# A fused sparse-attention and feed-forward kernel: a new written-out order, one zeroing moved from VectorE to GpSimd, fewer products without use

## The chip, the cores and the metric

The kernel runs on one core of a Trainium2 chip. The core has a matrix engine (TensorE, PE in the profile), VectorE (DVE), ScalarE (ACT), GpSimd (POOL) and SyncE (SP), which each work through their own list of instructions in order and wait for one another by semaphores; DMA queues move data between the memory outside the core (HBM) and its SBUF. Products land in PSUM, which has eight banks. The metric is the device time of one launch in microseconds. Three runs of the kernel before are shown; their median is the time before.

## The reference, cut to what matters

```python
# q, k, v: 4 batches x 8 heads x 768 positions x 64
k_sum = k.reshape(B, H, 24, 32, D).max(axis=3)       # block maxima of the keys
v_sum = v.reshape(B, H, 24, 32, D).mean(axis=3)      # block means of the values
scores_l = scale * q @ k.T                           # only |i - j| < 16 counts
scores_s = scale * q @ k_sum.T + log(32)
a = softmax(concat([where(mask_l, scores_l, -1e9), scores_s]))
x = (a @ concat([v, v_sum])).transpose(0, 2, 1, 3).reshape(3072, 512)
h = x @ w_in                                         # 512 -> 2048
out = (h * clip(h + 3, 0, 6) / 6) @ w_out            # 2048 -> 512
```

All inputs and the output are float32 in HBM; the kernel works in bf16 with float32 sums in PSUM.

## The kernel before

**Tiles and stages.** Of each batch, a block of 64 queries sees a window of 96 keys (its own 64 and 16 to either side) and the 24 block keys: 120 keys, on 120 partitions. So the values of two buffers, `vaug`, have 96 window rows and 24 rows of block means for each of 8 heads and 12 query blocks. The names carry the batch: `V0c` loads the values of head pair c of batch 0 (line 424, on POOL's queue) into rows 32 to 95. The window's first 32 rows are copied from other blocks (`h0cx`, "halo", line 427, x for the half of the query blocks). The block means of batch 0 come from `vsum_first` (`u00` and `u01`, line 612, two head pairs each): 24 products for each pair with a matrix `ind` of zeros and ones, 96 rows by 12 x 32 columns, whose ones mark which block a row belongs to. Rows 0 to 31 of `ind` must be zero, since the halo rows are counted in their own place. The sums are copied to `vf` and spread from there over the query blocks of `vaug`. `blocks()` (line 340) makes `ind` on POOL in three steps, and a DVE memset (line 347) zeroes its first 32 rows.

Keys and queries of a pair are loaded (`K0c`, `Q0..`), transposed on PE (`k0c`, `q0nc` steps, lines 495, 538, 551) and copied out of PSUM by DVE or ACT. A score step `s` (lines 579, 588) makes the scores of a pair in an `S` pair of banks, ACT takes their exponential into `at` (line 597) and DVE multiplies by `mask` (line 601). A value step `v` (lines 709, 711, 713) multiplies by the values and by a column of ones, and a finish step divides (lines 743, 747: reciprocal and scale on DVE into `xn`), transposes on PE (line 781) and copies to `x`. All small copies go through one helper, line 479.

Then, for each of 8 half batches s and 16 column blocks of `w_in`, step F (line 792) makes 4 products of 128 x 384 into a PSUM bank `h` (line 800), a relu on ACT (line 805) and a combined minimum and multiply on DVE into `g` (line 807). For the first half batch and the first blocks the products come in three parts of 128 columns, since the columns of `x` come one after the other. Step G (line 811) sums over the 16 `g` for 128 tokens into bank `o`, or `h` in the last half batch (line 820), copies to `ot` (line 479) and stores (line 832). The last tiles are stored in two halves of 256 columns.

**What sets the order.** All steps are registered with planned costs. A string `ORDER` (line 29) lists every step once, as a name, a running number and, where two engines could do it, the engine (`:A` ACT, `:D` DVE, `:P` POOL, `:S` SP). `Plan.run` (line 156) walks that list with a clock for each engine, the planned costs and the buffers that come free, which gives each step a planned begin and its buffers; the program is then written out in the order of the planned begins. Each engine keeps to its part of that order. The planned costs thus set the order and the choice of buffers, and nothing else. The loads of weights, keys, queries and values all go through POOL's queue; stores go through SP's, and some through POOL's.

**Products without use.** `keep` (line 907) writes products of a constant tile `idle` into a free bank (line 910). The loop behind it (lines 914 to 926) looks at each PE step that is planned before 22 us and puts as many of them ahead as the planned gap holds: by 0.43 us for one in the first 4.5 us, by 0.43 or by 0.216 after that.

Of the kernel before, what the change touches and what calls it, by code (L numbers as in the profile page):

```python
# [43 lines left out]
F13.9 F10.3 F13.10 F10.4 F10.5 F13.11 w13.0 G02.2 F10.9 F11.9 F10.10 F10.11 G02.3 F11.6 F12.3 w10.0 w12.0 w11.0 w12.1:D
G02.4:A F12.4 F11.10 w11.1:A G01.0 G01.1 G01.2 G01.3 u1.0 F11.11 G01.4:A F12.5 w11.2 w13.1:A F11.7 w10.1:A u1.1:A u1.6:A
w10.2 w13.2 w10.3:A u1.4:D F11.8 w13.3:D w11.3:D G00.0 G00.1 G00.2 q100.0 q120.0 q110.0 q100.1:A s100.0 s100.3 s100.1 G00.3
q130.0 q120.1:D q110.1:D w12.2 w12.3:D s100.2 u1.8:D u1.2:D s100.4 q130.1:D K23.0 h11.0 K22.0 h10.0 K21.0 Q21.0 K20.0 Q20.0
Q23.0 Q22.0 V22.0 h21.0 V21.0 h20.0 V20.0 V23.0 G00.4:A s110.0 G00.5 F13.3 G12.0 s110.1 s110.3 s120.0 F13.4 s120.3 s120.1
G12.1 G12.2 F13.5 u1.3:D s120.2 s110.2 h1w.0:A s130.0 s130.1 s130.3 G12.3 G12.4:A G12.5 G01.5 s130.2 s110.4 v10.0 s130.4
v10.1 v10.2 v10.5 v10.6 G11.0 G11.1 v12.0 v10.3 u1.9:A u1.7:A u1.5:A v12.1 v12.2 s120.4 w20.0 w20.3 G11.2 v10.4:A v10.7  # L50
v10.8:A v12.3 v12.4:A G11.3 v15.0 v15.1 v15.2 F20.0 G11.4:A F20.1 F20.3 F20.4 F20.6 v13.0 F20.7 F20.2 F20.5 F20.8 v13.5
v13.1 v13.2 F20.9 F22.0 F21.0 w20.2:A F20.10 F22.1 v13.3 F21.1 F20.11 F22.2 F21.2 w20.1 v13.6 F21.6 F22.6 F21.3 v13.4:A
F21.7 F22.7 v15.3 G10.0 v13.7 F21.4 v15.4:A w20.5:A v13.8:A F21.8 F22.8 F21.5 F22.3 F21.9 w20.4:A F22.4 F21.10 F22.9 G10.1
s200.0 w22.0 w21.0 F22.10 w22.2:A s200.3 s200.1 F22.11 F22.5 w23.0 F21.11 G10.2 F23.6 G10.3 F23.0 F23.3 V30.0 V33.0 V31.0
h30.0 h31.0 V32.0 Q33.0 Q31.0 K33.0 Q32.0 K32.0 Q30.0 K31.0 K30.0 F23.7 w21.2:A w21.1 F23.8 G10.4:A F23.1 w21.5:A F23.4 u2.0
u2.1:A u2.2:A F23.9 w21.3 w21.4:D F23.5 w22.1 F23.2 G10.5 G02.5 F23.10 s210.0 F30.9 G20.0 s210.3 u2.4:A u2.5:D w23.1 F23.11
w22.3 G20.1 F30.0 F30.1 F30.10 s210.1 w22.5:A F30.2 w22.4:D F30.11 u2.3:D G20.2 F30.3 G20.3 F30.4 w23.5:A F30.5 w23.3 s210.2
F30.6 G20.4:A F30.7 s210.4 F30.8 s220.0 w23.2:A s220.3 s220.1 w23.4:A F31.3 F33.3 G22.0 u3.0 F31.4 u3.1:A F33.4 s220.4
s220.2 s200.2 F31.5 F32.6 F32.7 s200.4 F33.5 F32.8 s230.0 G22.1 F31.0 G22.2 h2w.0:A s230.1 s230.3 s230.2 s230.4 F32.3 v20.0
F31.9 F31.1 F31.2 v20.1 v20.4 v20.2 v20.5 u3.5:A F31.10 F31.11 F32.0 G22.3 v22.0 v25.0 v20.3 v22.1 v22.2 v22.3 v20.6 F31.6  # L60
u3.3:A G22.4:A F32.4 F31.7 F32.1 F31.8 F32.5 F32.2 w30.1 v22.5:P v22.7:P G21.0 G21.1 G21.2 F33.6 G21.3 F33.7 G11.5 G20.5:S
v22.6:S v22.4:S F33.8 F33.9 F33.0 F32.9 v25.1 w31.1 v25.2 G21.4:A F33.1 G21.5:P G22.5:S F32.10 F32.11 G32.0 G32.1 G32.2
F33.10 F33.11 F33.2 G32.3 h3w.0:A G32.4:A w30.0 w30.3 w31.5:A w30.2:A u3.4:A v23.0 w31.0 G30.0 G30.1 G30.2 F40.0 F42.9
w30.4:A v23.4 v23.5 v23.1 v23.2 v23.3 v25.3 F40.1 F42.10 F40.3 F40.4 F40.2 F42.11 F41.3 F40.5 v23.6 F40.6 F40.9 F41.4 F40.7
F40.10 F41.5 G30.3 G30.4:A F40.8 F40.11 w31.3 F43.9 w30.5:A F43.10 F41.9 F43.6 F41.10 F43.7 F43.11 F41.11 u3.2:A v25.4:S
v25.7:P v25.6:P G32.5:S v25.5:S G30.5:P G31.0 F41.0 F41.6 F43.8 w31.2:D w31.4:D w33.0 F42.6 F41.7 F41.1 F41.8 F42.7 w32.0
F41.2 F42.8 s310.0 G31.1 s310.3 s310.1 F42.3 G31.2 F43.3 F42.0 F42.4 w32.2:A F43.4 F42.1 F42.5 w32.3 F43.0 F43.1 F43.5 F42.2
# [152 lines left out]
def kernel(  # L220
# [83 lines left out]
    def const_ops():  # L304
# [42 lines left out]
        op("DVE", 0.2, lambda: nc.vector.memset(ind[0:BLK], 0.0), w=["ind"], prio=-78)  # L347
# [609 lines left out]
```

## Time and profile before

| | |
|---|---|
| runs shown, us | 220.47, 220.41, 218.79 |
| median, us | 220.41 |
| profiled execution, us | 218.78 |
| its span, us | 217.1 |
| PE busy, us | 207.0 |
| DVE busy, us | 165.0 |
| ACT busy, us | 136.9 |
| POOL busy, us | 91.0 |
| products without use recorded (line 910) | 17, 7.4 us |
| DVE memset of `ind` (line 347) | 14.16 to 14.38 us |
| V's fourth piece, issue to landing | 9.46 to 17.26 us |
| first product of F | 21.97 us |

The span goes from the first to the last instruction of one profiled execution; the time of that execution is 1.7 us longer. Busy times are of single engines and overlap. Positions are in us from the start of the span. A row such as "A <- B: 1.2, 1, 1.2" among the waits says that A stood idle for B, how long in all, how often, and the longest. A line of the chain has start, length and the work that the end hangs on. The digits show forty equal slices of the span in tenths (9 is 90% or more).

### The profile page before, as it was taken

Reading aid. Unit: us, or ns where it says so; the run is one execution under the profiler, and the core shown is the slowest. Engines: PE = TensorE matmul, PEld = TensorE weight load, DVE = VectorE, ACT = ScalarE, POOL = GpSimd, SP = SyncE. Lnnn points to the kernel's source line nnn. Section 1 sums busy time; section 2 is a strip of 40 time slices with the busy share of each in tenths; the row PEclk is TensorE's granted clock in tenths of the full one; section 3 lists DMA queues with packets and bytes.
Section 4 is the critical chain, followed back from the end, with each engine's and each line's share of the span. In section 5 each row is a group of like instructions: output and inputs, shape, how many; then the busy total and the mean of one; then the engine's idle time right before and its main releaser. Section 6 shows DMA issues by size and latency. Waiting matters only on the chain.

```text
span 217.1 us, 5338 instructions
## 1 busy us (share of the span) xinstructions
PE 207.0 (95%) x2124; PEld 116.4 (54%) x2151; DVE 165.0 (76%) x330; ACT 136.9 (63%) x271; POOL 91.0 (42%) x117
## 2 busy tenths in 40 slices
PE   6979899999999999999999999999999999999994
PEld 2546656554554565555555555545555555555543
DVE  6889999779798899988898898987865756163310
ACT  8687795664789688998844788963342344345301
POOL 7997944254697856527254073000542401100000
PEclk9999999999999999999999999999999999999999
DMA  5999999999999999999936045000540452100212
GB/s 75 159 155 182 205 207 184 168 138 155 106 125 154 190 148 151 131 204 156 107 35 142 0 77 95 3 0 3 130 91 15 107 90 57 51 0 0 97 51 98
DMA packets 129705, 23.03 MB, mean 106 GB/s; under 512 B 120816, under 2 KB 127152, under 8 KB 129680
## 3 DMA queue, kind: packets, MB, share of 16 engines
q0 software_dynamic: 112656, 17.34, 119.2%
q1 hardware_dynamic: 17024, 5.34, 10.1%
q8 instruction: 17, 0.28, 0.5%
q14 instruction: 8, 0.07, 0.1%
HBM read 29.62 MB, written 6.29 MB: 165 GB/s over the span
## 4 chain that ended last, share of the span: by engine, by line
PE 84%; POOL 4%; DMA 4%; DVE 4%; issue 2%; ACT 2%; POOLq 0%
PE h L800 37%; PE o L820 32%; PE h L820 5%; DMA vaug<-in_v_dram 4%; PE S L709 3%; PE S L588 2%; DVE g L807 2%; POOL vaug L424 1%; PE S L641 1%; POOL first L383 1%; PE S L781 1%; DVE at L601 1%; ACT at L597 1%; POOL first L391 1%; ACT ot L479 0%
## 5 line engine op out<-in xcount | busy, mean ns | idle before, releaser
L800 PE MATMUL h<-x,win 128*128 128x384 bf16 (+1 forms) x536 | 94.3, 319 | 1.3 <-DVE g L807 1.3
L807 DVE SCALAR_TENSOR_TENSOR g<-r,h 128x384 bf16<-128x384 f32 x128 | 67.6, 547 | 29.8 <-ACT r L805 27.5
L805 ACT ACTIVATE r<-h 128x384 f32<-128x384 f32 x128 | 60.6, 492 | 45.9 <-PE h L800 44.4
L820 PE MATMUL o<-wout,g 128*128 128x512 bf16 x312 | 79.0, 379 | 1.6 <-issue 0.5
L800 PEld LDWEIGHTS <-win 128*128 128x128 bf16 x536 | 49.6, 98 | 36.5 <-issue 1.9
L820 PEld LDWEIGHTS <-g 128*128 128x128 bf16 x400 | 38.0, 98 | 36.7
L769 POOL DMA_DIRECT2D x<-y x28 | 17.2, 622 | 40.9 <-issue 22.0
L597 ACT ACTIVATE at<-S 120x768 bf16<-120x768 f32 x32 | 24.7, 813 | 2.4 <-PE S L588 2.4
L424 POOL DMA_DIRECT2D vaug<-in_v_dram x16 | 15.1, 945 | 13.0 <-issue 3.9
L479 ACT COPY ot<-o 128x512 f32<-128x512 f32 x18 | 10.6, 587 | 13.0 <-PE o L820 12.0
L601 DVE TENSOR_TENSOR at<-at,mask 96x768 bf16<-96x768 bf16 x28 | 14.5, 547 | 2.2 <-ACT at L597 1.8
L747 DVE TENSOR_TENSOR xn<-S,rc 128x512 bf16<-128x512 f32 (+1 forms) x24 | 15.7, 661 | 0.5
L413 POOL DMA_DIRECT2D kraw<-in_k_dram x8 | 10.7, 1339 | 8.2 <-issue 4.2
L479 ACT COPY vaug<-vs 24x1536 bf16<-24x1536 bf16 (+1 forms) x10 | 12.1, 1212 | 0.2
L678 DVE TENSOR_REDUCE red<-kaug 128x24 bf16<-128x768 bf16 x12 | 11.1, 941 | 0.1
L820 PE MATMUL h<-wout,g 128*128 128x256 bf16 (+1 forms) x63 | 10.7, 325 | 0.1
L832 POOL DMA_DIRECT2D out_dram<-ot x7 | 4.0, 567 | 14.0 <-DVE ot L479 8.5
L588 PEld LDWEIGHTS <-kaug 64*128 64x128 bf16 x384 | 6.8, 95 | 5.5 <-issue 3.3
L709 PEld LDWEIGHTS <-at 120*64 120x64 bf16 x360 | 6.8, 111 | 4.5 <-issue 3.7
L588 PE MATMUL S<-qT,kaug 64*128 64x64 bf16 x384 | 8.8, 191 | 0.2 <-ACT qT L479 0.2
L910 PE MATMUL o<-idle 128*128 128x512 bf16 x17 | 7.4, 572 | 1.6 <-DVE idle L306 1.5
L709 PE MATMUL S<-vaug,at 120*64 120x65 bf16 x352 | 8.2, 197 | 0.1
(107 smaller groups left out, 181.9 us busy)
## 6 DMA issues: line engine op xcount, KB each, us to landing
vaug<-in_v_dram POOLq DMA_DIRECT2D x22, 192.0 KB, 11.1
out_dram<-ot SPq DMA_DIRECT2D x14, 256.0 KB, 3.1
win<-in_moe_w_in_dram POOLq DMA_DIRECT2D x4, 512.0 KB, 8.5
wout<-in_moe_w_out_dram POOLq DMA_DIRECT2D x4, 512.0 KB, 14.5
kraw<-in_k_dram POOLq DMA_DIRECT2D x8, 192.0 KB, 13.8
out_dram<-ot POOLq DMA_DIRECT2D x5, 256.0 KB, 2.4
first<-in_k_dram POOLq DMA_DIRECT2D x6, 192.0 KB, 6.3
first<-in_q_dram POOLq DMA_DIRECT2D x6, 192.0 KB, 9.0
```

What stands on the lines that cost most here:

```text
L424: op("POOL", 0.95, lambda: nc.gpsimd.dma_start(out=o[BLK:WIN, lo:hi, 0:D], in_=rows[:, lo:hi]), w=[("v", b % 2, c)], prio=prio, dma=1.25, ...
L479: {"ACT": nc.scalar.copy, "DVE": nc.vector.tensor_copy, "POOL": nc.gpsimd.tensor_copy}[eng](o, i)
L588: nc.tensor.matmul(X[p, half].slot[:, j, i * QB:(i + 1) * QB], kaug[p][rows, t], qT[rows, p, t * QB:(t + 1) * QB], start=not masked, stop= ...
L597: op("ACT", act(2 * HALF), lambda a=a, x=x: nc.scalar.activation(a, x.slot[0:KEYS, :, 0:HALF], AF.Exp, scale=scl), r=[x], w=[("at", p, hal ...
L601: op("DVE", 0.57, lambda m=m, half=half: nc.vector.tensor_tensor(m, m, mask[:, low(half):low(half) + HQ].unsqueeze(1).to_broadcast([WIN, 2 ...
L709: nc.tensor.matmul(y, a[:, cols], vaug[b % 2][0:KEYS, h, t, 0:D + 1], start=True, stop=True)
L747: nc.vector.tensor_tensor(o, src[..., 0:D], r.unsqueeze(len(r.shape)).to_broadcast(list(o.shape)), op=ALU.mult)
L769: QUEUE[eng].dma_start(out=xt[s].slot[32 * a:32 * a + 32].rearrange("p k (t c j) -> p (k t) c j", t=3, c=4)[:, :, c], in_=ys[s].slot[32 * ...
L800: nc.tensor.matmul(h.slot[:, lo * 128:hi * 128], w_in_sb[:, kt, ft * 128:(ft + 1) * 128], xt[s].slot[:, kt, lo * 128:hi * 128], start=(kt ...
L805: op("ACT", act(HALF), lambda: nc.scalar.activation(r.slot[:], h.slot[:, 0:HALF], AF.Relu, bias=0.5, scale=1.0 / 6.0), r=[h], w=[r], prio= ...
L807: op("DVE", dve(HALF), lambda: nc.vector.scalar_tensor_tensor(gt[s].slot[:, ft], r.slot[:], 1.0, h.slot[:, 0:HALF], op0=ALU.min, op1=ALU.m ...
L820: nc.tensor.matmul(o.slot[:, a:z], gt[s].slot[:, ft, ts * 128:(ts + 1) * 128], w_out_sb[:, ft, a:z], start=(ft == 0), stop=(ft == NFT - 1))
```

## The change

The list is written anew from its first token. In the first 25 us: all small memsets (`z`, `e`) stand ahead of the constant tile `idle` (`c.0`) on DVE; the first sums `u00` stand ahead of the last scores of the start and take a bank `h`; `h030` and `h020` are both ahead of `u01`; `h011` is on ACT; `u00.6` (a spread of block means) is behind the third `g`; `q011` is ahead of `q031`; the edges of the second `vaug` (before `c.9`, after `c.8`) come earlier. Later steps and the stores of the last tiles are in a different order too, and some copies and stores are on another engine.

`blocks()` has a third POOL step behind its two selects, a memset of the first 32 rows of `ind`, in place of the DVE step, so that the numbers of the `c` steps behind it go down by one. The planned DVE costs of a halo copy and of the spread's second half are larger. `keep`'s rule for the time after 7.2 us is dropped, so that all gaps after 4.5 us are filled by 0.43 us less 0.4, and no product without use stands ahead of the sums. The program then has 13 of them instead of 19. The numbers of all products with use are as before.

```diff
--- before.py
+++ after.py
@@ -27,59 +27,59 @@
 
 
 ORDER = """
-c.0 z1.0:A z3.1:A z0.1:A K00.0 z1.1:D e.3 z0.2 z2.0:D c.8 K01.0 c.1 K02.0 Q000.0 c.2 Q010.0 c.3 k00.0 z0.0:D e.1 z3.0:D c.4
-k01.0 V00.0 V01.0 V02.0 V03.0 c.6 Q01w2.0 Q01w1.0 I0.0 Q01w0.0 k01.2:A k00.1 e.0 k01.1 z2.2 z3.2 z2.1:D k01.4 z1.2 k03.0
-k00.3:A k00.2:A k01.3:A q010.0 q010.1:A q000.0 k02.0 q000.1:A k00.4 s000.0 q030.0 s010.0 q020.0 s000.1 s010.1 e.2 k03.1
-k02.1 h000.0:D h001.0:D k03.4 c.7 q020.1:D k03.3:A q030.1:A k03.2:A s000.2 s010.2 Q11w0.0 I1.0 I2.0 u00.0 k02.4 h010.0:D
-u00.2:A k02.2:A h021.0:D h020.0:D u00.1:D u00.3:D u00.5:D h030.0:D s030.0 s030.1 s020.0 s020.1 s030.2 u01.0 s020.2 I3.0 O0.0
-O1.0 K13.0 O2.0 O3.0 K11.0 K10.0 K12.0 u01.2:A u01.1:A v00.0 v01.0 v02.0 v01.1 v00.2 v00.3 v02.2 v02.3 v01.2 v01.3 v00.1
-v00.6 v02.1 v00.4 v00.5 v02.4 v02.5 k02.3:A v00.7:A u00.4:A v01.4 v00.8 v00.9:A v01.5:A v02.6 v02.7:A F00.0 F00.10 F00.1
-q021.0 q001.0 F00.2 q021.1:A h011.0:D u00.6:D h031.0:D u01.3:D q001.1:D F00.3 F00.11 F00.12 q031.0 F00.4 F00.5 F00.6 F00.7
-F00.15 q031.1:A F00.13 F00.8 F00.16 c.5 F00.14 F00.9 F00.17 u01.4:D s031.0 q011.0 s031.1 q011.1:A F01.6 F01.7 s031.2 F01.8
-F01.3 F01.4 F01.0 F01.1 F01.5 c.9 F01.2 s001.0 s011.0 s011.1 s011.2 s001.1 s001.2 F02.0 F02.9 F02.1 F02.2 s021.0 F01.9
-F02.10 F02.11 F03.0 F02.3 s021.1 F01.10 s021.2 F03.1 F01.11 v03.0 v04.0 F03.2 v03.1 v04.1 v04.2 v03.2 F03.6 F03.9 G02.0
-v03.3 v05.0 F02.4 F03.10 F03.7 F02.5 F03.8 v05.1 v05.2 F02.6 v03.4:A F02.7 v04.3 F03.3 v04.4:D Q11w3.0 V13.0 V12.0 V10.0
...
-F73.2 F70.9 F70.6 F70.7 F70.8 F72.0 G60.2 F72.1 F70.10 F70.11 F72.2 F73.6 F73.7 F73.8 G60.3 G60.4:A F71.9 F72.6 F72.7 F71.10
-F71.11 F72.8 G61.0 F70.3 F70.4 F70.5 G61.1 F73.9 F73.10 F73.11 F71.0 F71.1 F71.6 F71.7 F71.8 F71.2 G61.2 F72.3 F72.4 G61.3
-G70.0 G61.4:A F72.5 G62.5:P G61.5:S G71.1 G71.3 F73.3 F73.4 G70.1 G70.2 F73.5 G60.5:S G70.3 G72.0 G72.1 G70.4:D G70.5 G71.5
-G72.2 G72.3 G71.0 G71.2 G72.4:A G72.5 G71.9 G71.10:D G71.11 G71.4 G71.6 G71.7:A G71.8
+z2.2 z1.2 z3.2 e.3 e.0 c.0 z1.1:D z0.1:A z1.0:A z3.1:A K00.0 c.7 z0.0:D z2.0:D z3.0:D e.1 z0.2 K01.0 c.1 K02.0 Q000.0 c.2
+Q010.0 c.3 k00.0 c.4 k00.1 e.2 k00.4 k01.0 V00.0 V01.0 V02.0 V03.0 c.6 Q01w2.0 Q01w1.0 I0.0 Q01w0.0 k01.2:A k01.1 k01.4
+z2.1:D k03.0 k00.2:A k00.3:A k01.3:A k02.0 k02.2:A k03.1 k03.4 q010.0 q000.0 q010.1:A q000.1:A s010.0 q020.0 q030.0 k03.3:A
+q030.1:A s000.0 s010.1 s000.1 u00.0 s010.2 s000.2 k03.2:A k02.1 k02.4 h000.0:D h001.0:D q020.1:D h010.0:D u00.2:D u00.5:D
+h021.0:D u00.1:A u00.3:D h030.0:D h020.0:D Q11w0.0 I1.0 I2.0 s020.0 s020.1 s030.0 s030.1 u01.0 s020.2 s030.2 I3.0 O0.0 O1.0
+K12.0 O2.0 O3.0 K10.0 K13.0 K11.0 u01.1:A u01.2:A v00.0 v01.0 v02.0 v01.1 v00.2 v00.3 v02.2 v02.3 v00.6 v00.1 v01.2 v01.3
+v00.4 v00.5 v02.1 v02.4 v02.5 u00.4:A k02.3:A v00.7:A h011.0:A v01.4 v00.8 v00.9:A v01.5:A v02.6 v02.7:A F00.10 F00.0 F00.1
+q021.0 q001.0 F00.2 F00.11 F00.12 F00.5 q021.1:A h031.0:D u01.3:D u01.4:D q001.1:D F00.3 F00.13 q011.0 F00.6 q011.1:A q031.0
+F00.7 c.5 F00.8 q031.1:A F00.4 c.8 F00.14 F00.9 F00.15 s001.0 s031.0 F00.16 s031.1 u00.6:D F00.17 F01.6 F01.7 s031.2 F01.8
+F01.3 F01.4 s011.0 F01.0 F01.5 s001.1 s001.2 F02.0 F02.9 s021.0 F01.1 F01.2 F02.1 F02.2 s011.1 s011.2 F02.10 F02.11 F02.3
+F01.9 F03.0 s021.1 F01.10 s021.2 F03.1 F01.11 v04.0 v03.0 v04.1 F03.2 v03.1 v04.2 v03.2 F03.6 F03.9 G02.0 v05.0 v03.3 F03.7
...
+F70.8 F72.6 F72.7 F73.3 F73.4 F73.5 F72.0 F72.1 F72.2 F72.8 G60.3 F71.0 F71.9 G60.4:A F71.1 F71.2 F71.6 F71.7 F71.8 G61.0
+F70.3 F73.0 G61.1 G61.2 F70.4 F73.1 F73.2 F71.10 F70.5 F70.9 F70.10 F70.11 F71.11 G61.3 F73.9 F72.3 F72.4 G72.0 G72.1 F72.5
+F73.10 G62.5:S G61.4:A G61.5:P G60.5:P F73.11 G70.0 G72.2 G71.1 G71.3 G71.5 G71.9 G71.10:D G71.11 G51.5:P G70.1 G72.3
+G72.4:D G72.5 G71.0 G70.2 G70.3 G70.4:D G70.5 G71.2 G71.4 G71.6 G71.7:A G71.8
 """
 
 BANKS = ("S", "h", "o")
@@ -343,8 +343,8 @@
                                     pattern=[[QB, NQ], [-BLK, 32]])
             nc.gpsimd.affine_select(out=ind[:], in_=ind[:], compare_op=ALU.is_ge, fill=0.0, base=2 * BLK - 1, channel_multiplier=-1,
                                     pattern=[[-QB, NQ], [BLK, 32]])
-        op("POOL", 1.6, blocks, w=["ind"], prio=-78.5)
-        op("DVE", 0.2, lambda: nc.vector.memset(ind[0:BLK], 0.0), w=["ind"], prio=-78)
+            nc.gpsimd.memset(ind[0:BLK], 0.0)
+        op("POOL", 1.85, blocks, w=["ind"], prio=-78.5)
 
         def edges(i):
             t = vaug[i]
@@ -434,7 +434,7 @@
             copy(eng, o[0:BLK, hs, a:z, 0:D], o[QB:WIN, hs, a - 1:z - 1, 0:D])
             if x:
                 copy(eng, o[0:BLK, hs, 0, 0:D], o[QB:WIN, hs, NQ - 1, 0:D])
-        op(EITHER, {"ACT": 0.75 + 0.1 * x, "DVE": 0.42 + 0.1 * x}, go, r=[("v", 0, c), ("vz", 0, c)], w=[("vh", 0, c, x)],
+        op(EITHER, {"ACT": 0.75 + 0.1 * x, "DVE": 0.45 + 0.35 * x}, go, r=[("v", 0, c), ("vz", 0, c)], w=[("vh", 0, c, x)],
            prio=prio, after=LATER * x)
 
     def halos(b, prio):
@@ -626,7 +626,7 @@
                r=[T], w=[("vf", c)], prio=prio + 0.1)
         for c in cs:
             for x in (0, 1) if c < 2 else (1,):
-                op(EITHER, {"ACT": 0.8, "DVE": 0.4}, lambda eng, x=x, c=c: copy(
+                op(EITHER, {"ACT": 0.8, "DVE": 0.4 + 0.15 * x}, lambda eng, x=x, c=c: copy(
                     eng, vaug[0][WIN:KEYS, 2 * c:2 * c + 2, low(x):low(x) + HQ, 0:D],
                     vf[c][WIN:KEYS, :, 0:D].unsqueeze(2).to_broadcast([NB, 2, HQ, D])),
                    r=[("vf", c)], w=[("vsum", 0, c, x)], prio=late + c if x else prio + 0.2, after=LATER * x)
@@ -917,9 +917,9 @@
             if o.begin < SLOW:
                 n = int((o.begin - end) / 0.43 + 0.1 + (not first and any(d.dma for d in o.deps)))
             else:
-                n = int((o.begin - end) / 0.43 - 0.4) if end < 1.6 * SLOW else int((o.begin - end) / 0.216 + 0.5)
+                n = int((o.begin - end) / 0.43 - 0.4)
             idle_ = [s for s in banks if not any(a < o.begin and z > end and x is s for a, z, x in plan.lives)]
-            if n > 0 and idle_:
+            if n > 0 and idle_ and o.form != "sums":
                 last = o.begin
                 todo.append(lambda n=n, s=idle_[-1]: keep(n, s))
             end, first = max(end, o.end), False
```

More of the change, by code (lines that the diff above doesn't have):

```diff
@@ L44 @@
[L44 to L67, printed above, removed]
@@ new lines @@
+F12.7 F10.8 F10.5 F12.8 G02.2 F11.9 F12.3 G02.3 F11.10 w13.0 F11.11 F11.6 F13.6 G02.4:A G01.0 G01.1 G01.2 G01.3 w10.0 w10.2
+w12.0 w11.0 w10.1:A F11.7 F13.7 F12.4 w13.1:A G01.4:A w11.1:A u1.0 u1.1:A u1.8:A w10.3:D F12.5 F11.8 w13.2 w12.1:A G00.0
+G00.1 G00.2 q100.0 q110.0 q120.0 q100.1:A u1.3:D w11.2 w11.3:A u1.2:D F13.8 w13.3:D u1.6:D w12.2 s100.0 s100.1 s100.3
+q110.1:D w12.3:D q120.1:D G00.3 q130.0 s100.2 K22.0 h10.0 Q20.0 h11.0 K20.0 K21.0 K23.0 Q21.0 Q23.0 h21.0 Q22.0 V21.0 V23.0
+V20.0 V22.0 h20.0 G00.4:A s110.0 G02.5 G01.5 G00.5 F13.3 G12.0 s110.1 s110.3 s120.0 F13.4 s120.3 s120.1 G12.1 G12.2 h1w.0:A
@@ new lines @@
+F22.11 F23.0 F23.3 F23.6 w22.0 w21.3 G10.1 V33.0 V32.0 V30.0 h30.0 V31.0 h31.0 Q33.0 K32.0 K30.0 Q30.0 Q32.0 Q31.0 K31.0
+K33.0 w21.2:A s200.3 F23.4 F23.5 s200.1 F23.1 F23.7 w22.2:A u2.0 u2.1:A F23.9 w21.1 F23.10 w21.5:A w21.4:D u2.2:A F23.2
+F23.8 G10.2 F30.0 G10.3 F30.1 G10.4:A F30.9 G10.5 G12.5 F23.11 w22.3 u2.5:D F30.3 F30.10 u2.4:A s200.4 F30.2 w22.1 w22.4:D
+F30.11 w23.0 s210.0 s210.3 u2.3:D s210.4 w22.5:A s210.1 G20.0 G20.1 G20.2 G20.3 F30.4 G20.4:A F30.5 s220.0 s220.3 w23.3
+F30.6 F33.3 F31.3 u3.0 G22.0 F30.7 F33.4 s220.1 s220.4 F30.8 F33.5 w23.1 F31.4 s210.2 s220.2 F31.5 s200.2 F32.6 G22.1
@@ new lines @@
+w23.2:A u3.1:A w23.4:A w23.5:A s230.0 F31.0 F32.3 G22.2 F32.7 h2w.0:A F32.8 s230.1 s230.3 s230.2 s230.4 v20.0 F31.9 F31.1
+F31.2 v20.1 v20.4 v20.5 v20.2 F31.10 F32.0 F31.11 G22.3 v25.0 v22.0 v20.3 v22.1 v22.2 v20.6 v22.3 F31.6 F32.1 G22.4:A F31.7
+F32.4 h3w.0:A u3.5:A F32.5 F31.8 F32.2 w30.1 v22.7:P v22.5:P G21.0 G21.1 G21.2 G20.5:P G11.5 G22.5:S v22.6:S v22.4:S F33.6
+F33.0 G21.3 F33.7 F33.8 F32.9 F33.9 F33.1 w31.1 F33.2 v25.1 G21.4:A F32.10 F32.11 F33.10 F33.11 w31.0 v25.2 w30.0 G32.0
+G32.1 G32.2 G32.3 u3.4:A G32.4:A u3.3:A v23.0 v23.1 v23.2 v23.3 v23.4 w30.3 v23.5 v25.3 G30.0 G30.1 G30.2 F40.0 F42.9 F40.1
@@ new lines @@
+w33.5:A F50.7 s320.3 F50.8 s320.2 s310.2 F50.10 F50.11 G41.0 G41.1 G41.2 F51.9 s330.0 s330.1 s330.3 F52.0 G41.3 F51.0
+G41.4:A F52.1 F51.1 s330.2 s300.4 s320.4 s330.4 v30.0 v30.4 v30.5 F51.2 v30.1 F52.2 s310.4 v30.2 v30.3 v30.6 G42.0 G42.1
+G42.2 G42.3 F51.6 v35.0 v32.0 G42.4:A F51.10 G40.0 G40.1 F52.6 F52.7 G40.2 F51.7 v32.1 v32.2 v32.3 F51.11 v35.1 F52.8 F51.8
+G41.5:S v32.6:P v32.4:P v32.7:S v32.5:S G31.5:S F50.3 F53.6 F50.4 F53.7 F53.8 F50.5 v35.2 G40.3 F51.3 G40.4:A F52.3 F52.4
+F52.5 F53.3 F51.4 F51.5 F53.4 F53.5 G50.0 F52.9 F53.0 F53.9 F52.10 F52.11 F53.1 F53.10 F53.11 F53.2 G50.1 v33.0 v33.4 G50.2
@@ new lines @@
+G50.3 G50.4:A F61.3 F60.0 v33.1 v33.5 v33.2 v33.3 v35.3 F63.3 F61.4 F60.1 F60.2 F61.5 G52.0 F63.4 F63.5 F63.9 F62.9 G52.1
+F63.10 F62.10 F62.11 v33.6 F61.0 F61.1 F63.11 F61.2 G52.2 F60.3 F60.4 F61.6 F61.7 F61.8 F60.5 G52.3 v35.5:P G50.5:S v35.6:P
+v35.4:S v35.7:S G40.5:S G42.5:P G52.4:A G52.5:S F62.0 F60.6 F63.0 F62.1 F63.1 G51.0 G51.1 F62.2 F60.7 F60.8 F63.2 G51.2
+F61.9 F61.10 F62.6 F60.9 F60.10 F62.7 G51.3 F61.11 F60.11 G51.4:A F63.6 F62.3 F63.7 F62.4 F63.8 F62.8 F62.5 G62.0 F72.9
+F70.0 G62.1 F72.10 F70.1 F70.2 F72.11 F71.3 G62.2 G62.3 G62.4:A F73.6 F70.6 G60.0 G60.1 G60.2 F71.4 F70.7 F73.7 F71.5 F73.8
```

26 lines of the change are left out of this document (13 added, 13 removed).

## The prediction

> **What bounds the kernel now.** I read the page's shares first, then the waits of TensorE (PE), then the chain between 13 and 36 us, and last the rows of VectorE (DVE) and GpSimd (POOL) beside the two stretches that the chain names. From the page:
>
> ```profile
> PE 207.0 (95%) x2124; PEld 116.4 (54%) x2151; DVE 165.0 (76%) x330; ACT 136.9 (63%) x271; POOL 91.0 (42%) x117
> PE   6979899999999999999999999999999999999994
> PEclk9999999999999999999999999999999999999999
> PE 84%; POOL 4%; DMA 4%; DVE 4%; issue 2%; ACT 2%; POOLq 0%
> ```
>
> PE is busy for 207.0 of 217.1 us at an undiminished granted clock, and the chain that ends last is PE for 84%. The change takes out no product with use, so it can only win where PE stands. The waits of PE say where (us in total, times, longest):
>
> ```profile
> PE o L910 <- DVE idle L306: 1.5, 1, 1.5
> PE h L800 <- DVE g L807: 1.3, 2, 1.0
> PE o L620 <- DVE ind L347: 1.2, 1, 1.2
> PE o L820 <- issue: 0.5, 3, 0.2
> PE h L620 <- DVE vf L479: 0.3, 1, 0.3
> PE h L495 <- DMA first<-in_k_dram: 0.2, 1, 0.2
> PE S L588 <- ACT qT L479: 0.2, 1, 0.2
> ```
>
> After 34 us no wait of PE is over 0.22 us, and those that are no mere issue gaps sum to about 0.8. So two can be won: 1.25 us before the first sums (L620, at 14.44), and 1.04 before L800 at 25.69. The chain shows which of them counts:
>
> ```profile
> 9.46 7.81 DMA vaug<-in_v_dram
> 17.30 0.83 PE h L620 x23
> 18.63 0.32 PE o L910
> 21.52 0.38 PE o L910
> 24.69 0.36 DVE qT L479
> 25.08 0.56 DVE g L807
> 32.12 1.46 PE h L800 x8
> ```
>
> The 1.25 us isn't on it: the load of V's fourth piece is, which lands at 17.26 and lets the second sums go at 17.30. The 1.04 us is: the chain lies on DVE from 24.69 to 32.07 and on PE after that.
>
> **The change, part by part**, against the profiled execution (218.78 us; span 217.1 and 1.7 around it).
>
> *The zeroing of ind's first 32 rows.* On DVE it took 218 ns and ended at 14.38, behind halo copies. POOL has no row for 32 rows; its fill of all 96 (L341) took 437 ns, so I bound it by 0.22 and 0.44, and take 0.44 and a 0.07 gap as between the steps before it (the width is the same). It ends at 12.18 + 0.51 = 12.69. What is queued behind it on POOL, the loads from Q01w2 to I3, is issued 0.51 later. V03 is issued at 9.46, ahead of it. Those loads land 5.6 to 11.5 us after issue, while 160 to 207 GB/s flow, so the transfers and not the issues set their landing; and POOL stands 1.55 us at 21.34 waiting for one of them, where the 0.51 is given back. Cost 0; without that cover it would be 0.51 on the loads of weights, which F needs.
>
> The first sums then wait for other things, a halo copy on DVE and a qT copy on ACT, and start at 13.1 to 14.1, 0.35 to 1.3 earlier. The second sums still wait for V03. Next late is the same landing, so the value is **0**. The other three pieces took 5.8 to 6.4 us to land against 7.8. Had V03 landed at 15.7, PE of before could have begun at 16.96 (its wait for vf), PE of after at about 15.9: the other end is −1.0.
>
> *Products without use (L910)*: 19 become 13. The start keeps its 7 + 6. The one near 11.34, that ahead of the second sums, and those at 18.57, 20.87 and 21.52 (two) go. The last four lie on the chain with 0.21 to 0.38 us each, but only because DVE is not done: F's first product needs transposes of xn, which end on DVE at 21.68. Value 0 as long as DVE is as late. At the start DVE does five small memsets ahead of the one that the first product waits for, about 0.35 us; the seven then end near 5.0, against K00's landing at 4.90, and K01's at 5.87 takes up the 0.1.
>
> *DVE from 18.17.* Before, one halo copy (349 ns) lies ahead of the reciprocals and scalings, which run back to back to 21.68. After, it is two (h030, h020): one more such copy, 0.17 to 0.35 us. F starts at 21.97 before, and at 22.2 to 22.4 after. I take **+0.3**.
>
> *DVE from 21.7 to the late g.* Its rows before (start, length, with two copies in some):
>
> ```profile
> 21.71 0.59 DVE L479 COPY vaug<-vaug 32x640 bf16<-32x640 bf16 x2
> 22.31 0.70 DVE L479 COPY vaug<-vf 24x768 bf16<-24x768 bf16 x1
> 23.02 1.25 DVE L479 COPY vaug<-vaug 32x640 bf16<-32x640 bf16 x2
> 24.30 0.36 DVE L479 COPY vaug<-vf 24x768 bf16<-24x768 bf16 x1
> 24.69 0.36 DVE L479 COPY qT<-S 128x384 bf16<-128x384 bf16 x1
> 25.08 0.56 DVE L807 SCALAR_TENSOR_TENSOR g<-r,h 128x384 bf16<-128x384 f32 x1
> ```
>
> After, h011 (0.59) is on ACT and u00.6 (0.70) behind the third g. From 22.05 DVE does h031 (0.315 + 0.17), two vf copies (0.36 each), qT (0.39) and the mask (0.6, once behind the first g): the first g starts at 22.05 + 2.2 = 24.3 and ends 0.61 later, 24.9, in place of 25.69. But the copies have two lengths. The same form takes 0.34 to 0.36 or 0.70 to 0.77 us, the 32x128 one 0.17 or 1.01. The long ones are those that begin well inside a POOL issue of loads and end 0.1 to 0.2 us after it (1.01 us to 24.27, beside the issue of 22.80 to 24.29; 0.77 to 17.71, beside that of 16.69 to 17.52). The Trainium skill, "GPSIMD Engine Reference", 1. Specifications, says that GpSimd and VectorE share SBUF interfaces and contend when VectorE runs in a two-port mode. The rows agree: copies out of PSUM in the same stretch keep their 0.36 us. By that rule alone the gain here would be what the collision leaves, +0.0 to −0.7 in the sum below.
>
> The issue from 22.80 to 24.29 is there after as well, and meets a vf copy: up to +1.1 (to 25.45), in the usual case +0.35 to 0.6. I take g's end at 25.3. PE has 2.7 us of products from F's start, and one transpose of q more (0.17): it runs dry at 22.3 + 2.87 = 25.15. Its stand is then 0.15 (0 to 0.9) in place of 1.04. With F's +0.3 the stretch gives +0.3 − 0.9 + 0.2 for the other DVE work that now lies behind g (u00.6, another memset pair, between which before shows 0.21 of standing at 32.12): **−0.4**, from −0.8 to +0.2.
>
> *From 34 to 210 us.* Products are the same. Nothing but 0.8 us can be won, and any late g or copy costs up to what one cost at 25.69, 1.04. V's second batch goes ahead of one load of q by some 0.8 us, while the last q lands as before (56.85). Value 0, from −0.5 to +1.0.
>
> *The end.* Before, the last three stores land 2.02, 1.71 and 1.70 us after their issue, and the span ends 3.1 after the last product. After, the next-to-last store is one in two pieces behind a DVE copy (0.69); such a one took 2.36 before. It lands at the last product's end + 2.2 to 2.6, where the last 128 KB landed at + 2.13. **+0.1**, from 0 to +0.4.
>
> The halo's and the spread's other planned costs issue nothing; they changed the list only. Sum: −0.4 + 0.1 = **−0.3**, or 218.5. The runs shown are 218.79, 220.41 and 220.47; their median lies 1.6 above the profiled execution. That gap is not in the profile of a single execution. I take it as a property of the start which stays, two times in three: **219.9**.
>
> **The rivals.** (1) *It gains more*: V03 lands early in the changed kernel or no copy meets an issue. −0.8 at the late g and up to −1.0 at the sums: 218.78 − 1.5 = 217.3 in an execution like the profiled one, 218.9 in the others. For it: the other pieces' 5.8 to 6.4 us. Against: the queue is as full as before.
>
> (2) *Slower, by the clock of PE.* Products of 512 columns start 427 ns apart up to 9.3 us and 213 to 216 after. Without the idle products, PE in 14.6 to 22.2 us shows short transposes and standing (one stand of 1.4 us ahead of the second sums). Should the array fall back to the slow spacing there, the products that follow take twice as long for a stretch as long as that warm-up, 3.4 us from 5.9 to 9.3, of which half is lost: +1.7, up to +3.4 if it happens twice: 221.6 to 223.3. It decides when PE's busy share over such a stretch goes below what before shows there: 2.15 of 3.4 us in 11.2 to 14.6, with no fall. After, I count 1.9 to 2.1 between 13.9 and 17.3 (first sums 0.4 to 0.7, two sets of scores 0.72 each). For it: removed work, lower share. Against: the share stays near a value that did no harm. The Trainium skill, "TensorE: Matmul & The Clock Gate", "Why this matters for your kernels", asks for a gap of about 3 us before the clock falls; by that, 1.4 us does nothing and the sum stands.
>
> (3) *Slower, by the copy's collision*: the first g is later than before, since vf copies in the POOL issue last 1.0 each, and one later g in 34 to 60 us is missed for 1.0: 218.78 + 0.2 + 1.0 + 0.2, 220.2; or 221.8 in the others.
>
> (4) *It doesn't do what it says*: DVE's passes come no earlier, PE stands 1.0 before L800 still, F starts 0.3 later: +0.3, 220.7.
>
> **How the numbers follow.** Forecast 0.53; (1) 0.15; (2) 0.10; (3) 0.12; (4) 0.10. One per cent, 2.2 us, is about what can be told from no change, since the three runs alone differ by 1.7. Faster than 218.2 needs case (1) with an execution of the short kind, or the forecast with one and 0.3 more than its sum: 0.13. Slower than 222.6 needs (2) in its dearer form, or (3) with a second such stand after 34 us: 0.12. Same: 0.75. The range goes from 217.7, inside (1), whose shorter end it leaves out, to 222.1, which holds (3), (4) and the cheaper form of (2).
>
> **What would show it.** The first L620 starts at 13 to 14 us and the second at the landing of V03; the wait on ind is gone. L800's wait for g falls from 1.0 to under 0.5. F's first product begins 0.2 to 0.4 later. L910 counts 13 or one less. After 34 us no new wait of PE above 0.3. A 427 ns spacing anywhere after 10 us would show me wrong, as would V03 before 16.5, or a wait of PE on a copy or store in the last 60 us.

## The result

The changed kernel took 221.69 us (median of 20 runs, 219.98 to 223.04), the kernel before 219.08 (20 runs, 218.53 to 222.59). The ratio is 1.0109, with a 95% interval of 1.0089 to 1.0129: slower by 2.4 us by that ratio. The forecast of 219.9 stood on a kernel before of 220.41; it meant 0.5 us faster. Two of the three runs shown at first had been long ones; the median of 20 is 1.3 lower.

The profiled execution of the changed kernel took 222.95 us with a span of 221.2, 4.2 us more than that of before. From its page:

```profile
PE 207.9 (94%) x2120; PEld 117.6 (53%) x2145; DVE 164.2 (74%) x323; ACT 139.2 (63%) x277; POOL 92.4 (42%) x120
PE   6678999999999999997999999999999999999992
PEclk9958699999999999999999999999999999999998
PE 82%; DMA 6%; ACT 4%; issue 2%; DVE 2%; POOL 2%; SPq 0%; ACTq 0%; POOLq 0%
```

PE is busy longer, though six products without use were taken out, and the row of its clock is no longer all nines: in slices 3 to 5, between 11 and 28 us, it goes down to 5, 8 and 6 tenths. The waits of PE (us in total, times, longest):

```profile
PE o L910 <- DVE idle L306: 1.8, 1, 1.8
PE h L495 <- DMA first<-in_k_dram: 1.5, 2, 0.9
PE S L641 <- ACT at L597: 1.3, 1, 1.3
PE o L538 <- DMA first<-in_q_dram: 0.8, 1, 0.8
PE h L620 <- ACT at L597: 0.5, 1, 0.5
PE S L711 <- DVE vaug L479: 0.5, 1, 0.5
...
PE h L800 <- DVE g L807: 0.2, 1, 0.2
```

What the change was to win is won: L800's wait for g went from 1.3 to 0.2, the wait of L620 for `ind` is gone. But there is a wait of 1.3 us far behind (L641, at 102 us) which before doesn't have, and more standing between the transposes of K and q at the start.

Busy time of PE by stretches (start:end, length, PE busy with its number of products, granted clock, then DMA share and GB/s), the changed kernel:

```profile
8.50:11.90 3.40, 2.07 (x60) 0.99 1.85 162
11.90:18.60 6.70, 6.15 (x100) 0.50 2.16 165
18.60:22.20 3.60, 2.97 (x95) 0.97 1.76 174
22.20:25.50 3.30, 3.17 (x29) 0.50 1.25 208
25.50:28.90 3.40, 3.40 (x63) 1.00 1.24 205
```

Twice the clock is at half: for 6.7 us from 11.9 and for 3.3 us from 22.2. In the timeline the same work takes twice its time there. Before:

```profile
14.44 0.85 PE L620 MATMUL o<-vaug,ind 96*32 96x128 bf16 x24 [1.25 <-DVE ind L347]
21.96 0.84 PE L800 MATMUL h<-x,win 128*128 128x128 bf16 x12
```

and after (start, length, work):

```profile
14.43 1.47 PE L620 MATMUL h<-vaug,ind 96*32 96x128 bf16 x24 [0.55 <-ACT at L597]
23.61 1.49 PE L800 MATMUL h<-x,win 128*128 128x128 bf16 x12
```

The 24 sums take 1.47 instead of 0.85 us, F's first twelve products 1.49 instead of 0.84, and F begins 1.65 us later. The first product of G, which stands behind the same F work in both, comes at 37.3 instead of 35.5. At the end of the trace, 3.08 us lie between PE's last product and the end of the span before, and 4.09 after. There SP waits longer for stores (us in total, times, longest). Before:

```profile
SPq L952 <- DMA out_dram<-ot: 0.8, 1, 0.8
```

and after:

```profile
SPq L952 <- DMA out_dram<-ot: 1.4, 2, 1.1
```

So three theories: **the clock**, which falls for want of products without use; **the late order**, with its new wait at 102 us; **the end**. The runs take them one by one. The changed kernel's clock, as a mean over the span, was below 0.995 in 18 of its 20 runs.

### The profile page after: what moved, and what is told of

Same layout as the page of the kernel before. It is cut to its first block, busy times and chain, and to the rows that moved or that the text cites. A ratio compares the mean times of both kernels' runs of the same rounds, so it can differ in the third digit from the quotient of the medians.

```text
span 221.2 us, 5326 instructions
## 1 busy us (share of the span) xinstructions
PE 207.9 (94%) x2120; PEld 117.6 (53%) x2145; DVE 164.2 (74%) x323; ACT 139.2 (63%) x277; POOL 92.4 (42%) x120
## 4 chain that ended last, share of the span: by engine, by line
PE 82%; DMA 6%; ACT 4%; issue 2%; DVE 2%; POOL 2%; SPq 0%; ACTq 0%; POOLq 0%
PE h L800 36%; PE o L820 29%; PE h L820 5%; DMA out_dram<-ot 3%; PE S L588 3%; PE S L709 3%; DMA first<-in_q_dram 3%; ACT at L597 1%; PE S L641 1%; PE S L579 1%; PE S L781 1%; POOL first L383 1%; ACT ot L479 1%; ACT vaug L479 1%; PE h L620 1%
## 5 line engine op out<-in xcount | busy, mean ns | idle before, releaser
L800 PE MATMUL h<-x,win 128*128 128x384 bf16 (+1 forms) x536 | 94.0, 321 | 0.3 <-DVE g L807 0.2
L800 PEld LDWEIGHTS <-win 128*128 128x128 bf16 x536 | 50.3, 99 | 35.3 <-issue 0.9
L769 POOL DMA_DIRECT2D x<-y x32 | 19.5, 619 | 54.2 <-issue 22.1
L479 ACT COPY ot<-o 128x512 f32<-128x512 f32 x21 | 12.3, 587 | 18.6 <-PE o L820 15.6
L747 DVE TENSOR_TENSOR xn<-S,rc 128x512 bf16<-128x512 f32 (+1 forms) x24 | 15.5, 661 | 0.4
L832 POOL DMA_DIRECT2D out_dram<-ot x6 | 3.3, 560 | 27.9 <-ACT ot L479 27.9
L678 DVE TENSOR_REDUCE red<-kaug 128x24 bf16<-128x768 bf16 x12 | 11.2, 937 | 0.1
L588 PEld LDWEIGHTS <-kaug 64*128 64x128 bf16 x384 | 7.3, 98 | 6.9 <-issue 3.8
L588 PE MATMUL S<-qT,kaug 64*128 64x64 bf16 x384 | 9.4, 197 | 0.2 <-ACT qT L479 0.2
L762 DVE STREAM_TRANSPOSE y<-xn 128x512 bf16<-128x512 bf16 x12 | 8.1, 697 | 0.1
```

The source lines that it names most:

```text
L479: {"ACT": nc.scalar.copy, "DVE": nc.vector.tensor_copy, "POOL": nc.gpsimd.tensor_copy}[eng](o, i)
L588: nc.tensor.matmul(X[p, half].slot[:, j, i * QB:(i + 1) * QB], kaug[p][rows, t], qT[rows, p, t * QB:(t + 1) * QB], start=not masked, stop= ...
L747: nc.vector.tensor_tensor(o, src[..., 0:D], r.unsqueeze(len(r.shape)).to_broadcast(list(o.shape)), op=ALU.mult)
L769: QUEUE[eng].dma_start(out=xt[s].slot[32 * a:32 * a + 32].rearrange("p k (t c j) -> p (k t) c j", t=3, c=4)[:, :, c], in_=ys[s].slot[32 * ...
L800: nc.tensor.matmul(h.slot[:, lo * 128:hi * 128], w_in_sb[:, kt, ft * 128:(ft + 1) * 128], xt[s].slot[:, kt, lo * 128:hi * 128], start=(kt ...
```

## The experiments

Each was compared with the kernel before on the same chip. Ratios are of the time to that; 0.0046 is 1 us.

**The old rule for the products without use, on the new order.**

```diff
-                n = int((o.begin - end) / 0.43 - 0.4)
+                n = int((o.begin - end) / 0.43 - 0.4) if end < 1.6 * SLOW else int((o.begin - end) / 0.216 + 0.5)
...
-            if n > 0 and idle_ and o.form != "sums":
+            if n > 0 and idle_:
```

> The changed kernel with the old rule for the products without use, which on the new order writes 25 of them (the changed kernel 13, the kernel before 19). Theory A, the clock: after 9 us the granted clock stays at 1.00 or within 0.005 of it, and the time falls from 221.7 to 220.0 to 220.6, that is, to the kernel before plus the 1.3 us that PE stands at 102 us. Theory B, the low clock is no cause of the loss: time 221.7 or more, as twelve more products of 0.216 us lie on PE, up to 2.6 us: 221.7 to 224.3.

220.44 us (219.87 to 221.55), ratio 1.0062 (1.0038 to 1.0085). Twelve products more made the kernel 1.0 us faster by the ratios, and the clock was 0.998 or above in every run. The same stretches:

```profile
8.50:11.90 3.40, 2.90 (x61) 1.00 1.92 167
11.90:18.60 6.70, 5.58 (x125) 1.00 2.13 164
18.60:22.20 3.60, 3.04 (x76) 1.00 1.77 167
22.20:25.50 3.30, 3.30 (x55) 1.00 1.26 207
```

From 11.9 to 18.6 us PE does more products (125 for 100) in less busy time (5.58 for 6.15). In 8.5 to 11.9 it is busy for 2.90 of 3.40 us, where the changed kernel had 2.07 ahead of its first fall. Theory A holds. G's first product is at 35.3 us, 0.15 ahead of before; PE's last product is at 214.05 us (before 213.99). The 1.1 us by which this profiled execution (219.87) is still longer lies nearly all behind it, at the end.

What makes the clock fall is less plain. In the changed kernel's trace the granted clock changes at 11.86, 18.68, 22.10 and 25.51 us, once or twice 3.41 us apart. The two stretches of that length just ahead of its falls, in the columns of the table above:

```profile
8.44:11.86 3.42, 2.03 (x60) 1.00 1.83 163
18.68:22.10 3.42, 2.79 (x94) 1.00 1.79 173
```

The second fall came although PE was busy for 2.79 of 3.42 us. And the clock held behind stretches with less busy time, here in the runs with half of the products and with the new order from 40 us on (both below):

```profile
5.96:9.37 3.41, 1.93 (x22) 1.00 1.23 172
5.65:9.06 3.41, 2.02 (x26) 1.00 1.12 166
```

These two hold six products without use of 512 columns each; the two ahead of the falls hold transposes and other products of at most 384. But in the run with G12's store moved (below), the clock held behind a stretch without any of them and fell behind the next, which was busier:

```profile
15.36:18.78 3.42, 2.20 (x62) 1.00 1.82 173
18.78:22.19 3.41, 2.55 (x58) 1.00 1.82 174
```

So the busy time of PE alone doesn't tell when the clock falls, and what does is not settled here. That the missing products bring the falls, and that the falls cost time, is what the runs show.

**The new rule on the old order.** The same two lines the other way round, in the kernel before; 13 products.

> The kernel before with only the new rule for the products without use, 13 instead of 19. Theory A, taking them away lets the clock fall: granted clock of 0.97 to 0.99 in most executions and 219.1 becomes 220.3 to 221.0. Theory B, it takes the longer stands of the new order too: clock 1.00, and 218.8 to 219.2, since the six products lay beside VectorE's work.

218.72 us (218.59 to 220.65), ratio 0.9999 (0.9972 to 1.0027). The clock was below 0.995 in 7 of 12 runs, and the time is unchanged: theory B's time, with theory A's clock in part. Four of the seven took 219.4 to 220.65 us, but three of them 218.6 to 218.9, about what the five with a clock of 1.00 took (218.6 to 218.7). So a fall doesn't always cost; that it is free where PE would be waiting anyway is a guess. The interval leaves room for 0.6 us either way. A loss clear of noise was seen only where the new early order and the fewer products came together.

**Half of the products.** The changed kernel with the old rule up to a planned 15.5 us: 4 products ahead of q's transposes and 2 ahead of the second sums, 19 in all.

```diff
-                n = int((o.begin - end) / 0.43 - 0.4)
+                n = int((o.begin - end) / 0.43 - 0.4) if end < 1.6 * SLOW or o.begin > 15.5 else int((o.begin - end) / 0.216 + 0.5)
...
-            if n > 0 and idle_ and o.form != "sums":
+            if n > 0 and idle_ and (o.form != "sums" or o.begin < 15.5):
```

> The changed kernel with 6 products without use more, all ahead of the second sums (3 and 1 ahead of the transposes of q, 2 ahead of the second sums), so 19 as in the kernel before. Theory A, the clock's fall is settled by the stands up to 17 us: clock 0.995 to 1.00 and 0.8 to 1.2 us below the changed kernel's. Theory B, the stretch from 18 to 22 us settles it: clock 0.98 to 0.99 as without them, 0 to 0.4 us below.

220.88 us (219.64 to 221.95), ratio 1.0070 (1.0045 to 1.0096): 0.85 us of the 1.0 is back with six of the twelve. But the clock is below 0.995 in 7 of 9 runs still, 0.992 at the median where the changed kernel has 0.984. Neither theory by itself: the time is theory A's, the clock lies between. Where the falls that are left lie is not known, since the profiled execution (0.997) has none. The interval overlaps widely with that of the run with all twelve, and a little with the changed kernel's, so the 0.85 is a rough figure.

**The new order up to some 40 us, the old one behind it.** The list is the changed kernel's up to the loads of batch 1's values; what is left follows in the order of before. Once with 25 products, once with 13.

```diff
 ... v04.3 v05.3 F03.11 v04.4:D
-V13.0 V10.0 V12.0 V11.0 Q11w4.0
+F02.7 Q11w3.0 V13.0 V12.0 V10.0 V11.0 Q11w4.0
...
```

> The new order up to the loads of batch 1's values (about 40 us), the kernel before's order behind it, and the old rule for the products without use (25 of them). Theory A: the clock stays at 1.00 and the late g's 0.8 us are won, 0.3 of them lost to a later start of F: 218.97 becomes 218.3 to 218.7. Theory B, the new early order loses elsewhere (the stands before K02's and the second sums) what it wins at g: 218.9 to 219.8.

> The same as the kernel with 25 products without use, new order up to about 40 us and old order behind it, but with the new rule, 13 of them. Theory A, the missing products let the clock fall on the new order: clock 0.975 to 0.99 and 1.0 to 1.4 us more than with 25, 219.6 to 220.4. Theory B, they cost or give nothing here, as they did with the old order: the same as with 25 within 0.3 us.

With 25: 219.02 us (218.50 to 219.84), ratio 0.9992 (0.9968 to 1.0015). With 13: 219.91 us (218.86 to 221.39 but for one run of 271.51, which is left out of the ratio), ratio 1.0040 (1.0018 to 1.0062). The clock was below 0.995 in 1 of 12 and in all of the other 11 runs. So theory B has the time with 25, and theory A time and clock with 13. This is the cleanest price of the missing products: 0.0048, 1.05 us, as in the first experiment. And it says what the early order is worth by itself with the clock held: nothing that can be measured. By the trace with 25 products F starts at 22.66 (before 21.96), the wait for g is gone, and G's first product is at 35.13 (before 35.45), 0.3 us won there. That execution lost it again on the way:

```profile
39.11 11.02 DMA vaug<-in_v_dram
50.13 0.03 issue
50.16 0.98 DVE kaug L659
51.13 0.45 DVE g L807
51.59 0.04 issue
51.63 0.81 PE h L800 x4
```

This is the chain of waits. DVE's transpose of batch 1's keys waits for a landing at 50 us with a g behind it, and PE stands 1.2 us. In the profiled execution of before the last load of these keys had landed at 47.9 us; here it landed at 49.97. The chain names a load of V that landed beside it.

**The new order from some 40 us on.** The kernel before with the zeroing on GpSimd, and the changed order behind the loads of batch 1's values.

```diff
 ... v04.3 F03.3 v04.4:D
-Q11w3.0 V13.0 V12.0 V10.0 V11.0
+v05.3 F03.11 V13.0 V10.0 V12.0 V11.0
...
```

> The kernel before with the zeroing on GpSimd and the new order only behind the loads of batch 1's values (from about 40 us on). Theory A, the loss after 40 us is PE's stand at 102 us: 219.1 + 1.3 = 220.4 with a clock of 1.00 and a wait of L641 of 1.0 to 1.4 us. Theory B, all of the loss lies in the first 26 us: 218.9 to 219.3.

220.28 us (219.65 to 222.72), ratio 1.0071 (1.0045 to 1.0097), 1.55 us. The clock was below 0.995 in 4 of 12 runs. Theory A has the time but not the place: L641 waits only 0.08 us in this trace. The end is what differs: 4.10 us behind PE's last product in place of 3.08. The other 0.5 us of the loss isn't explained. 0.0071 and the 0.0040 of the early part with 13 products make 0.0111, the changed kernel's 0.0109.

**The store of G12.** In the changed order, from the chain:

```profile
93.05 0.59 ACT ot L479
93.64 0.02 issue
93.66 0.34 SPq L831
94.00 0.05 issue
94.05 6.50 DMA out_dram<-ot
100.55 0.02 issue
...
100.65 0.16 ACT ot L479
100.81 0.32 issue
101.14 0.83 ACT at L597
101.96 0.04 issue
102.00 0.85 PE S L641 x48
```

ACT copies G10's sums to an `ot` buffer at 93.05, and its two-piece store lands at 100.55. The next copy is to go to the same buffer, since the stores of G12 and G11 are listed behind G10's and hold the other two. It waits 3 us, the exponential queued behind it on ACT too, and that holds the bank `S` which L641 is to write. Before, two other stores stood behind G10's as well (G02's and G11's), but its copy was at 87.66 and the next at 96.38, far enough apart.

```diff
 G12.4:A
+G12.5
...
 G10.5
-G12.5
```

> The changed kernel with the store of tile G12 listed right behind its copy, as in the kernel before, instead of 130 steps later. Theory A: the copy of G20 at 98 us finds a free buffer and no longer waits for the landing of G10's store; the 1.3 us that PE stands ahead of L641 at 102 us go, 221.7 becomes 220.4, and the clock below 1.00 in 11 to 26 us stays. Theory B, another stand comes up in its place (a store in the way of loads, or the bank held by another copy): 221.4 to 222.

221.05 us (219.77 to 221.88), ratio 1.0082 (1.0054 to 1.0111): 0.6 us won, which is not clear of noise by itself (the changed kernel has 1.0089 to 1.0129), and no wait of L641 is left in the list of waits. The copy now runs as PE delivers:

```profile
97.15 0.58 ACT L479 COPY ot<-o 128x512 f32<-128x512 f32 x1 [0.53 <-PE o L820]
```

All six runs kept a clock of 0.976 to 0.992, as theory A had it; the time lies between the two theories. That the price is half of the 1.3 us fits with a wait that isn't always as long: it was 0.27 us in the first experiment, 0.57 with half of the products, 0.74 below.

**The end.** The last rows of SP, in us behind PE's last product:

| | before | after |
|---|---|---|
| store before the last landed | 1.33 | 2.19 |
| last store landed | 2.14 | 2.52 |
| SP's last wait for stores ended | 2.18 | 2.72 |
| SP's closing drains | 2.25, 2.31 | 2.77, 3.21 |
| end of the span | 3.08 | 4.09 |

The last 128 KB take 2.09 us from issue to landing beside a store of 256 KB in two pieces that lands 0.33 us before them; before, they took 1.71, beside a store of 128 KB that landed 0.81 us before them. SP waits for the stores one by one in a fixed list of semaphores, and the late ones come earlier in it: behind the wait for the last landing stand two more waits and the drains, where before the drains alone stood. And SP pauses for 0.44 us ahead of its 80th recorded instruction. In the kernel before, which has 85, the 80th follows the wait for the last landing, and the pause is hidden in it. In the changed one, which has 83 (four moves of x to GpSimd, two stores more on SP), it is a closing drain that everything waits for. The first try puts the last 9 us in the order of before:

```diff
 ... F71.6 F71.7 F71.8
-G61.0 F70.3 F73.0 G61.1
+G51.5:P F73.0 F73.1 F73.2 F70.9
...
```

> The changed kernel with the kernel before's order from tile G61 of the last but one half batch on, about the last 9 us. Theory A: the stretch from PE's last product to the end of the span goes back from 4.1 us to 3.1 and 221.7 becomes 220.5 to 220.9, with the low clock of the first 26 us still there. Theory B, only the landing of the last store counts, 2.5 us behind PE in place of 2.1: 221.3.

221.75 us (221.19 to 222.78), ratio 1.0123 (1.0094 to 1.0152): nothing won. The last store lands at 2.13 again, but this program has 84 recorded instructions on SP, the 80th lies right behind the last landing's wait, and the pause is still seen: 3.65 us. In this execution the 0.44 won went into a new stand of 0.49 us of PE at 199.8, ahead of an F where the two orders meet. Theory A is right on the landing only, and neither theory has the time.

**All three undone at once.** The changed kernel with the old rule for products (25), G12's store behind its copy, and two late stores from GpSimd to SP.

```diff
 G12.4:A
+G12.5
...
-G61.5:P G60.5:P
+G61.5:S G60.5:S
```

> The changed kernel with the old rule for the products without use (25), the store of G12 right behind its copy, and the stores of G60 and G61 on SP instead of GpSimd, which gives SP three more instructions. Theory A: the three causes add up. SP's pause of 0.44 us ahead of its 80th recorded instruction falls again into the wait for the last store, the stretch from PE's last product to the end is 3.6 to 3.7 us in place of 4.1, and the time is 1.0 + 0.6 + 0.45 below the changed kernel's: 219.0 to 219.4. Theory B, the pause belongs to the work and not to the count: 4.1 us, 219.5 to 219.9.

219.17 us (218.69 to 221.0), ratio 1.0009 (0.9987 to 1.0032). No loss is left that can be told from noise, as theory A had it. SP has 86 recorded instructions, the 80th falls into the wait for a store, and the end takes 3.46 us, 0.63 less than in the changed kernel; 0.38 of that excess over before stays, the last landing's 2.54. No run's clock was below 0.998.

**The zeroing on GpSimd alone**, in the old order:

```diff
-        op("POOL", 1.6, blocks, w=["ind"], prio=-78.5)
-        op("DVE", 0.2, lambda: nc.vector.memset(ind[0:BLK], 0.0), w=["ind"], prio=-78)
+            nc.gpsimd.memset(ind[0:BLK], 0.0)
+        op("POOL", 1.85, blocks, w=["ind"], prio=-78.5)
```

> The kernel before with the zeroing of ind's first rows on GpSimd alone. Theory A: the first sums start up to 1 us earlier, the second sums still wait for V's fourth piece, and the time stays 218.97 within 0.3. Theory B: PE's stand moves behind the first sums, where nothing without use covers it, and the clock falls in more executions: 219.3 to 220.

219.38 us (218.48 to 221.56), ratio 1.0022 (0.9993 to 1.0050). It isn't settled between the two. The memset takes 0.41 us; the first sums start at 13.62 in place of 14.44 and the last product of the second begins at 17.87 (17.91): that much is as in theory A. The clock was below 0.995 in 2 of 12 runs, so theory B's cause is not seen.

**A version to beat both.** The new order up to the loads `K2` of the third batch's keys, some 75 us, with the old one behind it, and 25 products. The first transpose of batch 1's keys stands further back in it.

```diff
 ... G00.3 q130.0 s100.2
-K22.0 h10.0 Q20.0 h11.0
+u1.4:D s100.4 q130.1:D K23.0 h11.0
...
```

> The new order up to the loads of batch 3's keys (some 75 us), the old order behind it, 25 products without use. In the kernel with the new order up to 40 us alone, DVE's first transpose of batch 1's keys (L659) waited for a landing at 50.0 us and held a g, for which PE stood 1.2 us; here it comes behind one F step more. Theory A: that stand goes, and 218.85 becomes 218.1 to 218.5, with no execution above 219.5. Theory B: the landing varies by 2 us whatever the order, and the stand moves: 218.7 to 219.3.

The loads meant are those of K2, the third batch. 219.09 us (218.69 to 220.77), ratio 0.9998 (0.9974 to 1.0022). The stand at 51 us is gone, and still nothing is won: theory B. The profiled execution (220.77) has PE stand for only 3.75 us in all, against 6.98 before, and began its first sums at 16.0 instead of 14.4, with K's third load landing at 9.9 us instead of 9.1. No version here is faster than the kernel before.

## Why the prediction was wrong

The 2.4 us are some 1.0 for the clock (two pairs of kernels, 1.03 and 1.05), about 0.6 for the store (one run, not clear of noise by itself) and 1.0 for the end (by the traces, 4.09 us for 3.08; one experiment took 0.63 of it back). That is 2.6; the 0.2 too many lie within the noise. With all three undone, the one in part, no loss was left. The steps one by one:

- **The sums and V's fourth piece: right.** With the clock held, the first sums start at 13.6 to 14.7 us and the second end where they did (18.0 to 18.3, before 18.1), behind the landing of V03 (16.9 to 17.4 in all traces); the last version, where all began later, is the exception. The gain of the zeroing is hidden, as forecast; that it costs nothing on GpSimd's queue is not shown.
- **The late g: right, F's start mis-sized.** The wait fell from 1.04 to between none and 0.4 in the traces with 25 products. F's start was put at +0.3, and is +0.55 to +0.7 in three of these (in the fourth all began later). The stretch was to give −0.4; at G's first product it is −0.1 to −0.3.
- **"Value 0 as long as DVE is as late", for the products without use: wrong.** This is the step that failed first. It priced the six products by their place on the chain, not by what they do for the clock; rival (2) had the cause, with a chance of 0.10 and 1.7 us, and the runs show 1.0. Its point of decision was wrong. It took 11.2 to 14.6 us of before (2.15 of 3.4 us busy, no fall) as proof that 1.9 to 2.1 would do no harm, as if the busy time alone decided. The changed kernel fell behind 2.03 of 3.42 and again behind 2.79, and in other traces nothing fell behind 1.93, 2.02 and 2.20. Also the stretch was looked for around the second sums; the first fall came earlier, behind waits for the third load of K and the second of q (0.63 and 0.77 us), in whose places the profiled execution of before had no stand, with products without use ahead of them. They vary with the landings: the run with the old early order and the new late one had 1.30 ahead of K's third load, and no fall there. The page of the Trainium skill cited there, "TensorE: Matmul & The Clock Gate", asks for gaps of some 3 us, and no gap in front of the first fall was longer than 0.90. Its Part 1, "What's actually happening", speaks of a free-running window of some 3.4 us in which activity is counted. The rows agree with the window (falls of 6.8 and 3.4 us, two and one of it, in other places from run to run), and not with a limit on single gaps. What in such a window keeps the clock can't be read from these runs.
- **"Value 0" from 34 to 210 us: wrong.** The wait of one late operation was allowed for, up to +1.0, but as a bound and not as the likeliest. The stores' order was in the list to be read: three `ot` buffers, the stores of G11 and G12 behind G10's. The prediction didn't follow the buffers; a store took 6.5 us to land there.
- **"+0.1" for the end: wrong by 0.9.** The landing was bounded at +0.4 and came at +0.38. What the term left out is the closing: 0.2 for the order of the semaphores and 0.44 for a pause that the old program hid.
- **The base.** The 1.6 us between the profiled execution and the median was taken as staying two times in three. Of 78 runs of the kernel before beside the experiments, 59 kept a clock of 0.995 or more, with a median of 218.8, and 19 did not, with 220.1: much of that gap goes with the clock, and it stays one time in four. The 219.9 also doesn't follow from its terms: 218.5 is 220.1 with the whole gap and 219.6 with two thirds of it. That the measured 221.69 lies beside the 221.6 of rival (2) is luck: the clock cost 1.0 and not 1.7, the store and the end made up the difference, and the base was 1.3 too high.

## What to carry to other kernels

A product without use is no filler to be costed by its place on the critical chain: look at the stretches of some 3.4 us that it stood in, and at the work behind them that would run at half speed. PE's busy share there doesn't decide by itself, so read the granted clock of several executions, and run the kernel once with the products put back. When an order is written anew, follow every buffer of the stores to its next writer with the landing time of a store of the same stretch, not with the planned one. And count the instructions behind the last landing: what an engine does there is on the path of everyone.

## What was not expected of the hardware

- The clock fell to half with single stands of PE of no more than 0.90 us, behind 3.42 us in which PE was busy for 2.03, and again behind 2.79; with twelve short products more it did not. In other traces it held behind 1.93 and 2.20 of 3.4 us: busy time alone doesn't settle it.
- A fall need not cost: in the old order with 13 products, three runs with a mean clock of 0.992 took 218.6 to 218.9 us, much like those at 1.000, and two with the same mean took 220.5 and 220.6.
- SP pauses for 0.44 us ahead of its 80th recorded instruction in programs of 83 and 84 instructions, where the pause is in plain sight; with 85 and 86 the 80th follows a wait for a store. The Trainium skill, "Runtime: NRT & Kernel Launch", "Instruction fetch mechanics", says that engines fetch their instructions in blocks ahead of need and that this is normally hidden. Whether the pause is such a fetch is open: in the changed kernel's trace no DMA packet at all is recorded between 219.92 and 220.34 us, while SP pauses. That it goes by the count fits all six traces with 83 or 84 instructions, and the one with 86 that was made to try it.
- The same last store of 128 KB took 1.71 us beside one of 128 KB and 2.09 beside one of 256 KB in two pieces.
